# Block 0 by halves of the heads, and block 2's q and k transposes ahead of its V

## The chip, the cores and the metric

The kernel runs on one core of a Trainium2 chip. The core has a matrix engine (TensorE, PE in the profile, with its weight loads shown as PEld), a vector engine (VectorE, DVE), a scalar engine (ScalarE, ACT), GpSimd (POOL) and SyncE (SP), which here only issues transfers. Each engine works through its own list in order; semaphores order them against each other. Transfers run on 16 DMA engines that all issuing engines share. The metric is the device time of one execution in microseconds, and the median of the runs is compared.

## The reference

```python
# q, k, v: [8 batches, 8 heads, 576 tokens, 64], float32
q_c, k_c, v_c = (x.reshape(B, H, 9, 64, D) for x in (q, k, v))     # chunks of 64 tokens
scores = np.matmul(q_c, k_c.transpose(0, 1, 2, 4, 3)) / np.sqrt(D)
attn = np.exp(scores - np.max(scores, axis=-1, keepdims=True))
attn = attn / (np.sum(attn, axis=-1, keepdims=True) + 1e-09)
x = np.matmul(attn, v_c)                 # -> [4608 tokens, 512], heads side by side
h = np.maximum(x @ w_in, 0.0)            # w_in: [512, 2048]
out = h * h @ w_out                      # w_out: [2048, 512]
```

Attention runs only inside chunks of 64 tokens; then every token passes through two large products with a squared ReLU between them.

## The kernel before

**Tiling.** The 4608 tokens are cut into 18 groups of 256 (four chunks of one batch; the left-over chunks form two groups of their own), and two groups make a block of 512 tokens. The attention of a block must be done before its input projection, which goes over 16 d_ff tiles of 128 (each with four matmuls over d_model, `dt` 0 to 3); the output projection follows. The attention of later blocks is woven into the projections of earlier ones by hand: a loop hands out *slots*, one for each d_ff tile or output step, and a table `plan` says which attention steps, loads and sums come behind which slot. Blocks 0 to 3 use plain input projections; from block 4 on, and for most output projections, sums of operands replace one product in eight.

**One group's attention.** q and k arrive as float32, and TensorE reads the upper halves of the words as bf16. Groups 0 to 3 have q and k transposed on TensorE (`transpose_paired`, L400) and copied out of PSUM (L409); later groups have them cast on POOL (`cast_q`, `cast_k`, L449 and L454) and transposed by a DMA (`transpose_qk_dma`, L460). `scores` (L483) multiplies keys by queries and ACT takes the exponential (L494). `values` (L510) multiplies by V, which has a column of ones for the sums; DVE takes reciprocals (L442) and scales (L443). `transpose_x` (L540) or `transpose_x_early` (L521) brings x into the layout `xT` of the projection.

**PSUM.** Banks come round robin from two pools: `ps_ffn` with four, and the attention's two double banks (`att_bank`), which alternate.

**Block 0** has nothing to hide behind, and is written out before the slot loop. SP's list begins with q and k of groups 0 and 1, each 512 KB in runs of two rows of 64 (512 B), then V in 9 pieces, then w_in in eight loads of 256 columns (L329), each cast to bf16 on POOL (L334; the second half of the first on ACT, L333), then w_out (L339). PE goes through the two groups one behind the other, with `keep_busy` matmuls (L433, their result unused) in the gaps, and starts the input projection (`ffn_in`, L579) with d_ff tiles 0 and 1 on the first 256 tokens, then on the others, then goes on with 512 tokens at a time. ACT applies the ReLU (L590), and DVE or ACT squares (L598, L596).

**The slots of blocks 0 and 1.** In block 0's loop the q, k and V of block 2 (groups 4 and 5) are issued in the first 17 slots. In block 1's loop group 4 is cast at slot 16 and group 5 at slot 20 (`C`), their transposing DMAs come at 21 and 25 (`TD`), scores at 36 and 37, values at 38 and 40. As SP's list runs in order, the order of these lines is the order of the transfers.

## Time and profile before

| | |
|---|---|
| median of 3 runs | 277.18 us (277.12 to 279.81) |
| the profiled execution | 276.91 us, its span 275.1 us |
| busy over the span | PE 264.9 us (96%), DVE 199.2, ACT 168.3, POOL 89.6 |
| moved by DMA | 55.60 MB, mean 202 GB/s |
| chain that ended last | PE 87%, DMA 4%, SP's list 3%, DVE 3%, ACT 1% |

The span runs from the first to the last instruction of one execution. A profile row gives start and length in us, the engine, the line of the kernel, the operation, what it writes and reads with the shape, and in brackets how long the engine had been idle and what ended that. "PE busy" counts pipelined matmuls whose ends are modelled, so it is read together with the time per matmul.

### The profile page before, as it was taken

To read this page: it belongs to the slowest core of one execution; us is meant where nothing else is said; L and a number is where in the kernel's file an instruction comes from. 1 tells how busy PE (TensorE), PEld (TensorE's weight loads), DVE (VectorE), ACT (ScalarE), POOL (GpSimd) and SP (SyncE) were. 2 spreads that over 40 slices of the span, in tenths; PEclk is the share of its full clock that TensorE was granted. 3 is DMA by queue.
4 is the path that set the end of the run, shared out by engine and by line. 5 is a ranking of instruction groups with operands and counts; after the bars stand their busy time and mean duration, and the time that the engine had idled before them with its cause. 6 is when DMAs were issued, how large, how long until landed. Compare 5 with 4: busy or idle time off the path is not lost.

```text
span 275.1 us, 7923 instructions
## 1 busy us (share of the span) xinstructions
PE 264.9 (96%) x3261; PEld 203.4 (74%) x3261; DVE 199.2 (72%) x365; ACT 168.3 (61%) x300; POOL 89.6 (33%) x122
## 2 busy tenths in 40 slices
PE   2999999999999999999999999999999999999995
PEld 2764445888774588447878888888888888888884
DVE  1457514999538592499989998799779877994752
ACT  1657614894458883877678765565746665756430
POOL 2048834240360012040245224551643212331600
PEclk9999999999999999999999999999999999999999
DMA  7999999999999999999999999697999530220223
GB/s 216 262 352 389 361 332 270 339 213 172 262 210 218 238 234 218 275 223 178 228 236 197 218 238 194 103 220 196 244 187 224 123 76 2 99 55 7 71 83 114
DMA packets 136056, 55.60 MB, mean 202 GB/s; under 512 B 104273, under 2 KB 131921, under 8 KB 136017
## 3 DMA queue, kind: packets, MB, share of 16 engines
q1 hardware_dynamic: 133248, 46.54, 74.0%
q0 software_dynamic: 2624, 8.39, 9.6%
q8 instruction: 26, 0.43, 0.6%
q10 hardware_dynamic: 144, 0.13, 0.1%
q14 instruction: 14, 0.11, 0.1%
HBM read 36.70 MB, written 9.44 MB: 168 GB/s over the span
## 4 chain that ended last, share of the span: by engine, by line
PE 87%; DMA 4%; SPq 3%; DVE 3%; ACT 1%; issue 1%; ACTq 0%; DVEq 0%
PE ps_ffn L657 22%; PE ps_out L780 22%; PE ps_ffn L579 17%; PE ps_ffn L780 14%; PE ps_ffn L901 5%; PE ps_att L510 3%; PE ps_att L540 2%; DMA vo_sb<-in_v_dram 2%; PE ps_att L483 2%; DMA xT<-x 2%; DVE gT L598 2%; SPq L266 1%; SPq L308 1%; SPq L312 1%; DVE x L443 1%; ACT e L494 1%
## 5 line engine op out<-in xcount | busy, mean ns | idle before, releaser
L579 PE MATMUL ps_ffn<-xT,w_in_bf 128*128 128x512 bf16 (+1 forms) x328 | 57.8, 333 | 0.0
L780 PEld LDWEIGHTS <-w_st 128*128 128x128 bf16 x512 | 48.9, 98 | 6.6 <-DVE w_st L614 0.5
L665 DVE CUSTOM_DVE_ANT_0 relu<-ps_ffn,w_st 128x512 f32<-128x512 f32 x60 | 39.3, 684 | 13.0 <-PE ps_ffn L657 11.6
L579 PEld LDWEIGHTS <-w_in_bf 128*128 128x128 bf16 x328 | 31.2, 98 | 21.6 <-POOL w_in_bf L334 0.2
L598 DVE TENSOR_TENSOR gT<-relu 128x256 bf16<-128x256 bf16 (+2 forms) x68 | 34.1, 537 | 17.8 <-ACT relu L590 17.3
L590 ACT ACTIVATE relu<-ps_ffn 128x256 bf16<-128x256 f32 (+2 forms) x82 | 39.4, 501 | 9.4 <-PE ps_ffn L579 8.6
L657 PE MATMUL ps_ffn<-qk_st,w_in_bf 128*128 128x256 bf16 x240 | 35.3, 273 | 0.1
L657 PEld LDWEIGHTS <-w_in_bf 128*128 128x128 bf16 x320 | 30.7, 98 | 4.1 <-issue 0.3
L809 POOL DMA_DIRECT2D out_dram<-o_sb x24 | 17.6, 733 | 43.6 <-DVE o_sb L614 23.3
L780 PEld LDWEIGHTS <-gT 128*128 128x128 bf16 x296 | 28.6, 98 | 3.3
L780 PE MATMUL ps_out<-w_out_bf,w_st 128*128 128x256 bf16 x240 | 30.8, 273 | 0.0
L699 ACT ACTIVATE w_st<-ps_ffn 128x512 f32<-128x512 f32 x20 | 11.9, 597 | 29.6 <-PE ps_ffn L657 29.6
L443 DVE TENSOR_TENSOR x<-ps_att,recs 128x512 bf16<-128x512 f32 x36 | 24.9, 692 | 1.2
L657 PEld LDWEIGHTS <-qk_st 128*128 128x128 bf16 x240 | 22.6, 98 | 3.2 <-DVE qk_st L614 0.3
L657 PE MATMUL ps_ffn<-xT,qk_st 128*128 128x256 bf16 x160 | 23.9, 273 | 0.0
L676 POOL TENSOR_TENSOR qk_st<-relu 128x512 bf16<-128x512 f32 x10 | 10.3, 1034 | 41.6 <-DVE relu L665 38.1
L494 ACT ACTIVATE e<-ps_att 128x1024 bf16<-128x1024 f32 x18 | 18.3, 1025 | 8.5 <-PE ps_att L483 8.5
L676 POOL TENSOR_TENSOR gT<-relu 128x512 bf16<-128x512 f32 x10 | 10.3, 1033 | 35.4 <-DVE relu L665 30.5
L449 POOL CAST qkb<-qk_st 128x1024 bf16<-128x1024 f32 x12 | 13.0, 1082 | 14.9 <-DMA qk_st<-in_q_dram 14.9
L674 ACT ACTIVATE gT<-relu 128x512 bf16<-128x512 f32 x28 | 17.7, 631 | 0.0
L780 PE MATMUL ps_ffn<-w_out_bf,w_st 128*128 128x256 bf16 x144 | 17.7, 273 | 0.0
L614 DVE TENSOR_TENSOR w_st<-gT,w_st 128x1024 bf16<-128x1024 bf16 x26 | 16.8, 682 | 0.0
(92 smaller groups left out, 428.7 us busy)
## 6 DMA issues: line engine op xcount, KB each, us to landing
qk_st<-in_q_dram SPq DMA_DIRECT2D x16, 512.0 KB, 5.6
out_dram<-o_sb POOLq DMA_DIRECT2D x28, 256.0 KB, 3.9
qk_st<-in_k_dram SPq DMA_DIRECT2D x24, 256.0 KB, 5.6
ve_sb<-in_v_dram SPq DMA_DIRECT2D x32, 128.0 KB, 3.9
w_st<-in_moe_w_in_dram SPq DMA_DIRECT2D x8, 512.0 KB, 5.9
w_st<-in_moe_w_out_dram SPq DMA_DIRECT2D x8, 512.0 KB, 5.5
vo_sb<-in_v_dram SPq DMA_DIRECT2D x24, 128.0 KB, 3.6
qk_st<-in_k_dram SPq DMA_DIRECT2D x4, 512.0 KB, 5.8
```

What stands on the lines that cost most here:

```text
L443: nc.vector.tensor_tensor(out=x, in0=o[:, :, :, 0:D], in1=rec.to_broadcast([128, 2, n, D]), op=ALU.mult)
L494: nc.scalar.activation(out=e_out, in_=s_in, func=AF.Exp, scale=scale)
L579: nc.tensor.matmul(out=h[:, 0:n], lhsT=w_in_bf[:, dt, ft * 128:(ft + 1) * 128], rhs=xT[:, c // 128:(c + n) // 128, dt, :], start=(dt == 0) ...
L590: nc.scalar.activation(out=rl[:, 0:n], in_=h[:, 0:n], func=AF.Relu)
L598: nc.vector.tensor_tensor(out=dst, in0=src, in1=src, op=ALU.mult)
L614: nc.vector.tensor_tensor(out=out, in0=in0, in1=in1, op=op)
L657: nc.tensor.matmul(out=bank[:, f * GT:(f + 1) * GT], lhsT=a[:, dt, ft * 128:(ft + 1) * 128], rhs=b[:, :, dt, :], start=(first and f == 0 a ...
L665: nc.vector._custom_dve(TENSOR_ADD_SAT, out=out, in0=in0, in1=in1, s0=BIG, s1=0.0)
L674: engine.activation(out=dst, in_=r, func=AF.Square)
L676: engine.tensor_tensor(out=dst, in0=r, in1=r, op=ALU.mult)
L780: nc.tensor.matmul(out=out_ps, lhsT=lhsT, rhs=b[:, i, :], start=(first and i == 0 and (last or t == 0)), stop=(i == HF - 1), skip_group_ch ...
L809: dma.dma_start(out=out[t0:t0 + GT, col:col + HD].rearrange("(t p) d -> p t d", p=128), in_=o_sb.rearrange("p (t d) -> p t d", d=HD))
```

## The change

Block 0 is no longer done by its two groups of 256 tokens with all 8 heads, but by two halves of the heads (4 each) with all 512 tokens. For each half, q and k are loaded with four rows of 64 in a run (1 KB), V in 9 pieces of four heads, and w_in's first 512 columns in two halves of 256 rows, one behind each half's V. x of the first half of the heads is rows 0 to 255 of the projection's contraction (`dt` 0 and 1), so the first four d_ff tiles have these two matmuls done (`first_tile`) between the steps of the second half; `dt` 2 and 3 and the ReLU and square follow in `first_in` when the second half is done. Tile 3 of block 0 is squared on DVE in place of ACT. PE's fillers in the second half write into free columns of the attention's banks (`fill`).

In block 1's slots, the transposing DMAs of block 2 move from 21 and 25 to 16 and 20, directly behind their casts, and V of each of the two groups, until now issued in block 0's slots, comes behind its group's transpose, at 18 and 22.

```diff
@@ -312,10 +312,7 @@
             odd.append(lambda n=n, p=p, m=m, b=b, s=s: nc.sync.dma_start(
                 out=v_odd[n % NO][p:p + m, :, 0:D],
                 in_=v[b, 1::2, s:s + m, :].rearrange("h s d -> s h d")))
-        if g < 2:
-            yield from [even[0], *odd[:-1], even[1], odd[-1]]
-        else:
-            yield from even + odd
+        yield from even + odd
 
     def go(pieces):
         for f in pieces:
@@ -329,8 +326,6 @@
         nc.sync.dma_start(out=st, in_=moe_w_in[:, cols].rearrange("(a p) f -> p a f", p=128))
         n = 256 // n_cast
         for c in range(0, 256, n):
-            if i == 0 and c:
-                return lambda: nc.scalar.copy(out=w_in_bf[:, :, c:c + n], in_=st[:, :, c:c + n])
             nc.gpsimd.tensor_copy(
                 out=w_in_bf[:, :, i * 256 + c:i * 256 + c + n], in_=st[:, :, c:c + n])
 
@@ -514,18 +509,119 @@
                             start=True, stop=True)
             out_of_x(x[:, t].rearrange("p h a d -> p a h d"), ps, n_hp)
 
-    def transpose_x_early(g, t):
...
+    NH, HH = 2, H // 2
+
+    def half_loads(half):
+
+        b, s0 = chunks[0][0]
+        hs = slice(HH * half, HH * half + HH)
+
+        def rows(which, src):
+            return lambda: nc.sync.dma_start(
+                out=loaded(half, which).rearrange("p (h e) -> p h e", h=HH),
+                in_=src[b, hs, s0:s0 + BT, :].rearrange("h (s i) d -> s h (i d)", i=4))
+
+        def even(t):
+            s = s0 + 128 * t
+            return lambda: nc.sync.dma_start(
+                out=v_even[t // 2][:, t % 2, NH * half:NH * half + NH, 0:D],
+                in_=v[b, HH * half:HH * half + HH:2, s:s + 128, :].rearrange("h s d -> s h d"))
+
+        def odd(n):
+            p0, p1 = (CH if n == 0 else 0), (CH if n == 4 else 2 * CH)
+            s = s0 + 128 * n - CH + p0
+            return lambda: nc.sync.dma_start(
+                out=v_odd[n][p0:p1, NH * half:NH * half + NH, 0:D],
+                in_=v[b, HH * half + 1:HH * half + HH:2, s:s + p1 - p0, :].rearrange(
+                    "h s d -> s h d"))
+
+        return [rows(0, q), rows(1, k), even(0), even(1), odd(0), odd(1), odd(2), even(2), even(3),
+                odd(3), odd(4)]
+
+    def load_w_in_half(r):
+        st = w_st[next(n_staged) % 5].rearrange("p (a f) -> p a f", a=2)
+        nc.sync.dma_start(
+            out=st, in_=moe_w_in[256 * r:256 * r + 256, 0:512].rearrange("(a p) f -> p a f", p=128))
+        for c in (0, 256):
+            nc.gpsimd.tensor_copy(
+                out=w_in_bf[:, 2 * r:2 * r + 2, c:c + 256], in_=st[:, :, c:c + 256])
+
+    def transpose_half(half, which, bank):
...
+        qkT = state["half", half]
+        psb = bank.bitcast(BF16)[:, 0:1024].rearrange("c (h i q) -> c h i q", h=NH, i=4)
+        src = loaded(half, which).bitcast(BF16).rearrange("p (h i d) -> p h i d", h=HH, i=4)
+        for hp in range(NH):
+            for i in range(4):
+                for a in range(2):
+                    nc.tensor.transpose(
+                        out=psb[64 * a:64 * a + 64, hp, i, :],
+                        in_=src[:, 2 * hp + a, i, 1::2],
+                        identity=ident)
+        for hp in range(NH):
+            copy = nc.vector.tensor_copy if hp or not which else nc.scalar.copy
+            copy(out=qkT[:, which, hp].rearrange("c (p i) -> c p i", i=4),
+                 in_=psb[:, hp].rearrange("c i p -> c p i"))
+
+    def scores_half(half):
+        qkT = state["half", half]
+        ps = att_bank()
+        for hp in range(NH):
+            for t in range(4):
+                for a in range(2):
+                    for p in range(2):
+                        c = p ^ a
+                        o0 = a * 512 + hp * 256 + t * 64
+                        cols = slice((2 * t + p) * CH, (2 * t + p + 1) * CH)
+                        nc.tensor.matmul(
+                            out=ps[64 * c:64 * c + 64, o0:o0 + 64],
+                            lhsT=qkT[64 * a:64 * a + 64, 1, hp, cols],
+                            rhs=qkT[64 * a:64 * a + 64, 0, hp, cols],
+                            start=True, stop=True)
+        e = e_tile()
+        state["e half", half] = e.rearrange("p (a h t q) -> p a h t q", a=2, h=NH, t=4)
+        nc.scalar.activation(out=e, in_=ps, func=AF.Exp, scale=scale)
+
+    def values_half(half, u, n_fill=0):
+        e = state["e half", half]
...
+        x = state["x half", half]
+        ps = att_bank().rearrange("p (a f) -> p a f", a=2)
+        fill(n_fill, ps[:, 0, 384:512])
+        for tt in range(2):
+            t = 2 * u + tt
+            for hp in range(NH):
+                for a in range(2):
+                    for p in range(2):
+                        c = p ^ a
+                        vb = (v_odd[t + p] if a else v_even[t // 2][:, t % 2]).bitcast(BF16)
+                        o0 = (tt * NH + hp) * (D + 1)
+                        nc.tensor.matmul(
+                            out=ps[64 * p:64 * p + 64, a, o0:o0 + D + 1],
+                            lhsT=e[64 * c:64 * c + 64, a, hp, t, :],
+                            rhs=vb[64 * c:64 * c + 64, NH * half + hp, 1::2],
+                            start=True, stop=True)
+        out_of_x(x[:, 2 * u:2 * u + 2].rearrange("p t h a d -> p a (t h) d"), ps, 2 * NH)
+
+    def transpose_x_half(half, u, bank, copy):
+        psb = bank.bitcast(BF16)[:, 0:512]
+        x = state["x half", half]
+        for n in range(2 * NH):
             nc.tensor.transpose(
+                out=psb[:, n * 128:n * 128 + 128],
+                in_=x[:, 2 * u + n // NH, n % NH].rearrange("p a d -> p (a d)"),
                 identity=ident)
+        copy(out=x_tile(0)[:, 2 * u:2 * u + 2, NH * half:NH * half + NH, :],
+             in_=psb.rearrange("p (t h q) -> p t h q", t=2, h=NH))
+
+    def fill(n, out):
+        for _ in range(n):
+            nc.tensor.matmul(out=out, lhsT=ident, rhs=ident, start=True, stop=True)
 
     def transpose_x(g):
@@ -570,8 +666,26 @@
 
     FT_ORDER = [*range(n_ft // 2, n_ft), *range(n_ft // 2)]
 
+    def squared(j, u, h, c, n, ft):
+        gT = gT_main.rearrange("p (u h) (f t) -> p u h f t", u=2, f=4)
...
+        nc.scalar.activation(out=rl[:, 0:n], in_=h[:, 0:n], func=AF.Relu)
+        u0, u1 = c // GT, (c + n) // GT
+        dst = gT[:, u0:u1, ft // 4, ft % 4, :]
+        src = rl[:, 0:n].rearrange("p (u t) -> p u t", t=GT)
+        if (n == 512 and ft in SQUARES_ON_ACT and (j or ft > 3)) or (n < 512 and ft in (12, 3)):
+            nc.scalar.activation(out=dst, in_=src, func=AF.Square)
+        else:
+            nc.vector.tensor_tensor(out=dst, in0=src, in1=src, op=ALU.mult)
+
     def ffn_in(j, parts):
-        gT = gT_main.rearrange("p (u h) (f t) -> p u h f t", u=2, f=4)
         xT = xTs[j]
         for u, (c, n, ft) in enumerate((c, n, ft) for c, n, fts in parts for ft in fts):
             h = ps_ffn.tile([128, 512], FP32, name="ps_ffn")
@@ -581,23 +695,27 @@
                     lhsT=w_in_bf[:, dt, ft * 128:(ft + 1) * 128],
                     rhs=xT[:, c // 128:(c + n) // 128, dt, :],
                     start=(dt == 0), stop=(dt == n_dt - 1))
...
-            if (n == 512 and ft in SQUARES_ON_ACT) or (
-                    n < 512 and ft in (12, 3)) or (j == 0 and u == 0):
-                nc.scalar.activation(out=dst, in_=src, func=AF.Square)
-            else:
-                nc.vector.tensor_tensor(out=dst, in0=src, in1=src, op=ALU.mult)
+            squared(j, u, h, c, n, ft)
             yield
 
+    first_h = []
+
+    def first_tile(ft, dts):
+        if dts[0] == 0:
+            first_h.append(ps_ffn.tile([128, 512], FP32, name="ps_ffn"))
+        for dt in dts:
+            nc.tensor.matmul(
+                out=first_h[ft],
+                lhsT=w_in_bf[:, dt, ft * 128:(ft + 1) * 128],
+                rhs=xTs[0][:, :, dt, :],
+                start=(dt == 0), stop=(dt == n_dt - 1), skip_group_check=True)
+
+    def first_in():
+        for ft in range(4):
+            first_tile(ft, (2, 3))
+            squared(0, ft, first_h[ft], 0, BT, ft)
+            yield
+        yield from ffn_in(0, [(0, BT, range(4, n_ft))])
 
 
     a11, a12 = w_in_bf[:, 0:2, 0:d_ff // 2], w_in_bf[:, 2:4, 0:d_ff // 2]
@@ -964,33 +1082,40 @@
     def AV1(g):
         values(g, [1])
 
-    HT = BT // 2
-    go(pieces([0, 1]))
-    cast_first = load_w_in(0, n_cast=2)
-    TE(0)
-    transpose_qk(1, ps_ffn, None)
-    SC(0)
-    transpose_qk(1, None, ps_ffn)
+    def ffn_bank():
+        return ps_ffn.tile([128, 512], FP32, name="ps_ffn")
+
+    act = nc.scalar.copy
+    go(half_loads(0))
+    load_w_in_half(0)
+    go(half_loads(1))
+    load_w_in_half(1)
+    transpose_half(0, 0, ffn_bank())
+    transpose_half(0, 1, ffn_bank())
     keep_busy(8)
-    AV(0, [0])
-    SC(1)
-    keep_busy(6)
-    AV(0, [1])
-    transpose_x_early(0, 0)
-    keep_busy(10)
-    transpose_x_early(0, 1)
-    AV(1, [0])
-    AV(1, [1])
+    scores_half(0)
+    keep_busy(8)
+    values_half(0, 0)
+    values_half(0, 1)
     keep_busy(4)
-    transpose_x_early(1, 0)
-    cast_first()
-    keep_busy(8)
-    transpose_x_early(1, 1)
-    first_ffn_in = ffn_in(0, [(0, HT, (0, 1)), (HT, HT, (0, 1)), (0, BT, range(2, n_ft))])
-    next(first_ffn_in)
-    next(first_ffn_in)
-
-    for i in range(1, 8):
+    transpose_x_half(0, 0, ffn_bank(), act)
+    transpose_half(1, 0, ffn_bank())
+    transpose_x_half(0, 1, ffn_bank(), act)
+    first_tile(0, (0, 1))
+    transpose_half(1, 1, att_bank())
+    for ft in range(1, 4):
+        first_tile(ft, (0, 1))
+    scores_half(1)
+    values_half(1, 0, 8)
+    values_half(1, 1, 4)
+    both = att_bank()
+    fill(8, both[:, 256:384])
+    transpose_x_half(1, 0, both[:, 0:256], act)
+    fill(6, both[:, 256:384])
+    transpose_x_half(1, 1, both[:, 512:768], nc.vector.tensor_copy)
+    first_ffn_in = first_in()
+
+    for i in range(2, 8):
         load_w_in(i, n_cast=2 if i < 5 else 1)
     for i in range(5):
         load_w_out(i)
@@ -1009,7 +1134,7 @@
             plan.setdefault(slot, []).append((f, x))
 
         if j == 0:
-            loads, go_slots = pieces(far), range(17)
+            loads, go_slots = itertools.chain(*map(qk_pieces, far)), range(17)
             at(28, summed(b11_p_b21, b11, b21))
             for slot, f in ((24, TA), (27, SC), (29, AV), (31, XT)):
                 at(slot, f, nxt[0])
@@ -1022,9 +1147,10 @@
             for slot, f in ((3, SC), (6, AV), (12, XT)):
                 at(slot, f, grps[1])
             for i, g in enumerate(nxt):
-                for slot, f in ((16 + 4 * i, C), (21 + 4 * i, TD), (36 + i, SC), (38 + 2 * i, AV),
+                for slot, f in ((16 + 4 * i, C), (16 + 4 * i, TD), (36 + i, SC), (38 + 2 * i, AV),
                                 (41 + 2 * i, XT)):
                     at(slot, f, g)
+                at(18 + 4 * i, lambda g=g: go(v_pieces(g)))
             for i, g in enumerate(far):
                 at(36 + 4 * i, C, g)
                 at(42 + 3 * i, TD, g)
```

34 lines of the change are left out of this document (15 added, 19 removed).

## The prediction

> **What bounds the kernel now.** I read the page first: its span, and the rows of its 40 slices for TensorE (PE) and for the DMA engines.
>
> ```profile
> span 275.1 us, 7923 instructions
> ...
> PE   2999999999999999999999999999999999999995
> ...
> DMA  7999999999999999999999999697999530220223
> ```
>
> PE and the DMA engines both look full over most of the span, so the digits don't say which one sets the end. The busy times by stretch do, cut where block 0's first projection starts (17.46) and ends (31.47), and before the last stores.
>
> ```profile
> 17.46:31.47 14.01, 14.01 (x73) 7.17 (x74) 10.04 (x14) 10.84 (x22) 11.88 (x14) 1.00 1.06 379
> 31.47:260.00 228.53, 228.16 (x2841) 177.54 (x2840) 176.18 (x327) 146.84 (x262) 74.12 (x83) 1.00 0.85 193
> 260.00:275.10 15.10, 11.72 (x107) 10.05 (x104) 6.86 (x14) 3.14 (x9) 1.45 (x3) 1.00 0.36 110
> ```
>
> The columns are the length, then the busy time of PE, its weight loads, DVE (VectorE), ACT (ScalarE) and POOL (GpSimd). Of 228.53 us behind 31.47, PE is busy 228.16. A busy PE need not run at its peak, so I take the third view, the chain that ended last.
>
> ```profile
> 17.46 14.01 PE ps_ffn L579 x72
> 31.47 7.77 PE ps_ffn L901 x36
> ```
>
> 36 matmuls of 512 columns in 7.77 us are 0.216 us each. At that pace 64 such matmuls take 13.8 us, and the 64 tiles' worth of block 0's input projection took 14.01: PE runs without a gap from 17.46 on. So what a change of the opening is worth is how far it moves the moment at which this unbroken run of PE work reaches its 31.47, and a change behind that is worth something only where PE would wait.
>
> **The opening now.** I follow it in order of time.
>
> ```profile
> 4.77 1.06 PE L400 MATMUL ps_ffn<-ident,qk_st 128*64 128x128 bf16 x16 [4.77 <-DMA qk_st<-in_q_dram]
> 5.88 1.29 DVE L409 COPY qkT<-ps_ffn 128x512 bf16<-128x512 bf16 x2 [5.88 <-PE ps_ffn L400]
> 6.26 1.06 PE L400 MATMUL ps_ffn<-ident,qk_st 128*64 128x128 bf16 x16 [0.42 <-DMA qk_st<-in_k_dram]
> ...
> 8.74 0.64 PE L483 MATMUL ps_att<-qkT 64*64 64x64 bf16 x32
> 9.44 1.02 ACT L494 ACTIVATE e<-ps_att 128x1024 bf16<-128x1024 f32 x1 [1.00 <-PE ps_att L483]
> 10.36 1.03 PE L433 MATMUL ps_ffn<-ident 128*128 128x128 bf16 x8
> 11.32 0.30 PEld L510 LDWEIGHTS <-e 64*64 64x64 bf16 x16 [0.20 <-issue]
> 11.84 0.21 DVE L442 RECIPROCAL recs<-ps_att 128x8 f32<-128x8 f32 x1 [1.70 <-PE ps_att L510]
> 12.08 0.69 DVE L443 TENSOR_TENSOR x<-ps_att,recs 128x512 bf16<-128x512 f32 x1
> ...
> 16.30 0.69 DVE L443 TENSOR_TENSOR x<-ps_att,recs 128x512 bf16<-128x512 f32 x1
> 16.63 0.58 ACT L526 COPY xT<-ps_ffn 128x512 bf16<-128x512 bf16 x1 [1.38 <-PE ps_ffn L521]
> 17.05 0.40 PE L521 MATMUL ps_ffn<-ident,x 128*128 128x128 bf16 x4
> 17.48 0.42 DVE L526 COPY xT<-ps_ffn 128x512 bf16<-128x512 bf16 x1 [0.49 <-PE ps_ffn L521]
> ```
>
> The projection starts at 17.46 on the first 256 tokens, while the last copy of x for the others is still to come (17.48 to 17.90). The steps behind each arrival are thus partly covered now; in the new order the last group's steps are not.
>
> **When the data arrive.** The loads run in the order of SyncE's (SP's) list; the weight casts on POOL show their landings.
>
> ```profile
> 16.79 0.61 POOL L334 CAST w_in_bf<-w_st 128x512 bf16<-128x512 f32 x1 [14.59 <-DMA w_st<-in_moe_w_in_dram]
> 18.11 1.17 POOL L334 CAST w_in_bf<-w_st 128x512 bf16<-128x512 f32 x2 [0.70 <-DMA w_st<-in_moe_w_in_dram]
> 19.46 2.67 POOL L334 CAST w_in_bf<-w_st 128x512 bf16<-128x512 f32 x4 [0.18 <-DMA w_st<-in_moe_w_in_dram]
> ...
> 6.00:8.00 2.00, 1.31 (x22) 1.07 (x24) 1.17 (x2) 0.63 (x2) 0.00 (x0) 1.00 1.15 348
> 10.00:12.00 2.00, 2.00 (x65) 1.63 (x60) 0.30 (x2) 1.54 (x3) 0.00 (x0) 1.00 1.43 224
> ```
>
> 512 KB of q or k in runs of 512 B take 1.49 us (q at 4.77, k at 6.26). 512 KB of w_in in runs of 1 KB take 1.33 (16.79, 18.11, 19.46). V in runs of 256 B is slower: the last rows have 348 GB/s with q and k and 224 with V. From k of group 1 (6.26 and two more steps, 9.24) to the first w_in less its own 1.33 (15.46), 1 MB of V took 6.2 us. The change reads q and k by four heads in runs of 1 KB, so I price them at w_in's 1.33; V keeps its 256 B, 3.1 per half. Starting from 4.77 - 1.49 = 3.28, the new order lands q 4.61, k 5.94, V 9.04, w_in rows 0 to 255 10.37, then for half 1 q 11.70, k 13.03, V 16.13, and w_in rows 256 to 511 17.46. That is 0.65 ahead of the 18.11 of now for the same bytes. The Trainium skill (DMA: Bandwidth & Descriptors, Specifications) puts line rate at runs of 512 B and up; by that the longer runs of q and k gain nothing, and the start of the projection worked out below would be some 0.5 us later. The two rows, 1.49 against 1.33, speak for a small gain, and I keep it.
>
> SP must issue twice as many V pieces, 18 for 9, each of half the size.
>
> ```profile
> 0.75 0.45 SPq L266 DMA_DIRECT2D qk_st<-in_q_dram  x1
> ...
> 10.73 0.60 SPq L312 DMA_DIRECT2D vo_sb<-in_v_dram  x1
> ...
> 60.47 0.37 SPq L312 DMA_DIRECT2D vo_sb<-in_v_dram  x1
> ```
>
> An issue takes from 0.37 to 0.60 with 0.06 behind it. At 0.52 in all, SP is through V of half 0 at 6.6, through k of half 1 at 8.1 and V of half 1 at 12.8, and issues the second w_in half by 13.3: always ahead of the stream above. I take that, and keep 0.66 for a rival.
>
> **Block 0, step by step.** Half 0: k 5.94, 16 transposes 1.06, to 7.00; the two copies (0.65 each, now one on ACT and one on DVE) lie beside the 8 filling matmuls (1.03, to 8.03); scores start, exp 0.70 later (8.74 to 9.44), 1.02 long, to 9.75; the values then, reciprocal 0.52 behind their start (11.32 to 11.84), product 0.24 behind that, 0.69 long: 11.20; the second values' reciprocal and product follow on DVE, 0.03 + 0.24 + 0.69: 12.16. From here the machine is at its faster pace: the trace shows 128-column matmuls at 0.129 us at 10.36 and 0.072 at 13.32, and the same work later at
>
> ```profile
> 13.32 0.72 PE L433 MATMUL ps_ffn<-ident 128*128 128x128 bf16 x10
> ...
> 16.43 0.61 PE L433 MATMUL ps_ffn<-ident 128*128 128x128 bf16 x8
> ...
> 42.88 0.45 PE L483 MATMUL ps_att<-qkT 64*64 64x64 bf16 x32
> 43.38 1.02 ACT L494 ACTIVATE e<-ps_att 128x1024 bf16<-128x1024 f32 x1 [2.02 <-PE ps_att L483]
> ...
> 48.23 0.61 PE L400 MATMUL ps_ffn<-ident,qk_st 128*64 128x128 bf16 x16
> ```
>
> PE's list goes on with q of half 1: 11.70 + 0.61 = 12.31, just past the product; x of half 0's second part transposed, ACT's copy 0.44 behind its start and 0.58 long: 13.33. Only now can the first d_ff tile's two matmuls run (13.35 to 13.78), and behind them k of half 1, there since 13.03: to 14.39. Then the other three tiles' six matmuls, 1.30, to 15.69, which cover the copies of k (15.05). Scores 15.69; exp 0.50 later (42.88 to 43.38), to 17.21; values 17.25; reciprocal 17.77; products to 18.70 and 19.66; transposes 19.71; copy 0.43 behind their start, 0.42 long: **the projection proper starts at 20.6**, with w_in's casts long done (17.46 + two of 0.61). V of half 1 (16.13) is not what it waits for.
>
> Eight of its 64 matmuls are done by then. The remaining 56 at 0.216 take 12.1 and end at 32.7, against 31.47: **1.2 us later**. Break-even is a start at 19.4. What is gained (1.7 us of PE work laid into waiting time) is less than what is exposed: half 1's chain from scores to copy, 4.9 us in which PE has only filling matmuls. Nothing behind is late for it: w_in's third load lands near 18.8 and is needed at 22.3. The square of tile 3 moves from ACT to DVE and tile 0's comes to DVE whole, beside 12 us of PE work; DVE is busy 10.04 of 14.01 us in this stage, so I count nothing. Without that room it would be one pass over 128x512, near the copy's 0.42.
>
> **Block 2's transposes ahead of V.** SP's list now has V of groups 4 and 5 (to 61.6) ahead of the two transposing DMAs.
>
> ```profile
> 54.67 1.04 POOL L454 CAST qkb<-qk_st 128x1024 bf16<-128x1024 f32 x1 [2.69 <-DMA qk_st<-in_k_dram]
> 58.86 1.17 POOL L454 CAST qkb<-qk_st 128x1024 bf16<-128x1024 f32 x1 [1.61 <-DMA qk_st<-in_k_dram]
> ...
> 61.66 6.17 SPq L460 DMA_TRANSPOSE qkT<-qkb  x2
> ...
> 70.15 0.44 PE L483 MATMUL ps_att<-qkT 64*64 64x64 bf16 x32
> ...
> 73.93 0.22 PE L510 MATMUL ps_att<-ve_sb,e 64*64 64x65 bf16 x2
> ...
> DMA to landing us min/median/max: 2.4/3.9/7.2
> ```
>
> New: the first transpose waits for its cast (55.7) and issues to 58.8 (half of 6.17); behind it on SP wait five V pieces (near 0.55 each, 61.6), the second transpose (its cast ends 60.0, so no wait; 64.7) and four V pieces (66.9), then block 3's q and k, which before start at 67.9. No queue but SP's is passed, and nothing ends later on it. The last V piece lands at the median 3.9 behind its issue (66.4 + 3.9 = 70.3), at the longest 7.2 (73.6), and is used at 73.93 + 1.2. PE doesn't wait here before (scores at 70.15 directly behind the matmuls), so nothing is to gain: 0, from 0 to 0.8 lost with both the longest issue and landing. A gain needs a PE wait that isn't there.
>
> Sum: +1.2 us on the profiled execution's 276.91 (275.1 of span, 1.8 around it). It lies 0.27 under the median of the runs, 277.18; on that the forecast is **278.4**.
>
> **Rivals.**
> (a) Not slower: the DMA stream, not PE, sets what follows. Place: the loads from 17 to 200 us; price: they come 0.65 earlier, so 277.18 - 0.65 = **276.5**; it decides if PE's idle time behind 31.47 is over 1.2 us, so that the later start vanishes in waits. For it: the DMA row is at 9. Against: only 0.37 us of idle there. 0.07.
> (b) SP's issues bind. At 0.66 each, V of half 1 is issued to 15.5 and the second w_in half at 16.1; with q's 4.0 from issue to landing (0.75 to 4.77) that lands at 20.1, and the last V at up to 19.4 (3.9), 1.7 us late for the second values: **280.1**. For it: 0.60 at 10.73; against: 0.37 and 0.45 where fewer are outstanding. 0.13.
> (c) The half chain meets the slower pace: PE has more pauses between 10.5 and 13.5, and the first tiles are matmuls on the path. With 0.129 / 0.072 = 1.8 times on 8 of 0.216 (1.4 more), two sets of transposes (0.45 each) and the scores (0.64 for 0.45): 2.5 more, **280.9**. Against: the pauses in which PE waits for x and V now, from 13.3 to 16.4, left its pace as it was (0.072 at 13.32, 0.076 at 16.43). 0.10. The Trainium skill (TensorE: Matmul & The Clock Gate, Part 1) has a gate that opens after some 3.4 us of sustained work and shuts after an idle window as long; the trace agrees with the opening (slow at 10.36, fast at 13.32), and no run here shows a shutting.
> (d) The reordering doesn't do what it says: transposes come no earlier and V late, a wait of 0.8 at the values: **279.2**. 0.05.
>
> **How the numbers follow.** Forecast 0.62 (starts from 19.9 to 21.3 by 0.7 us of landings and gaps, 277.7 to 279.1), (a) 0.07, (b) 0.13, (c) 0.10, (d) 0.05, the rest 0.03 on either side. The range 276.5 to 280.8 takes in all but most of (c), half of (a) and the rest. About 1%, 2.8 us, is what a measurement here tells from no change: slower than 279.95 is half of (b), nearly all of (c) and little else, 0.17; faster than 274.4 has no case of its own, 0.02; within 1% 0.81.
>
> **What would show it.** Block 0's projection starting its second halves near 20.6, PE idle or filling from 16.2 to 20.1; first d_ff tile near 13.4; output projection from 32.7; the first block-2 transpose issued near 56; PE without gaps behind. The forecast is wrong if the second halves start before 19.4, if k of half 1 lands past 14, or if PE waits between 60 and 80.

## The result and the profile after

The changed kernel takes 284.75 us (median of 6 runs, 283.71 to 286.13) where the kernel before, on the same chip, takes 277.35 (6 runs, 276.47 to 279.81): 1.0257 times as long, 95% interval 1.0208 to 1.0307. The forecast was 278.4 with a range to 280.8. The profiled execution after took 283.71 us, 6.8 more than the one before (276.91). Here and below, medians and ranges are of all runs of a kernel, while ratios leave out the runs that fell into a slower state.

The chain that ended last and the stretches cut at the same events as in the prediction (start of the second halves of block 0's projection, start of the output projection, last stores) put all of the loss ahead of 25.86. The chain leads back to the load of q of half 1, issued at 7.64 and landed at 13.66:

```profile
7.64 6.02 DMA qk_st<-in_q_dram
...
25.86 1.89 PE ps_ffn L707 x8
```

The last three columns of a stretch are TensorE's granted clock (1.00 is full), the DMA share and GB/s.

```profile
25.86:37.95 12.09, 12.09 (x57) 5.48 (x57) 10.77 (x13) 9.14 (x16) 9.32 (x9) 1.00 0.98 339
37.95:260.00 222.05, 221.08 (x2776) 171.36 (x2778) 171.26 (x320) 143.47 (x255) 69.86 (x77) 1.00 0.87 196
```

The 56 matmuls of 512 columns take 12.09 us without a gap, and the output projection starts at 37.95, where the trace before has 31.30 for the same matmuls in the same view: 6.65 us later. Behind that point PE is idle 0.97 us in 222.05 (0.37 in 228.53 before). PE's last instruction ends 6.87 us later than before (278.59 against 271.72), so the remaining 0.2 us is all that the rest of the program adds. What has to be explained is why the second halves started at 25.86 and not at 20.6.

PE's timeline of the opening (start, length, engine, line, and in brackets the idle time before with what ended it):

```profile
13.71 1.06 PE L559 MATMUL ps_ffn<-ident,qk_st 128*64 128x128 bf16 x16 [1.62 <-DMA qk_st<-in_q_dram]
14.70 0.61 PE L615 MATMUL ps_ffn<-ident,x 128*128 128x128 bf16 x4
15.98 1.01 PE L707 MATMUL ps_ffn<-xT,w_in_bf 128*128 128x512 bf16 x2 [0.67 <-ACT xT L619]
16.93 1.06 PE L559 MATMUL ps_att<-ident,qk_st 128*64 128x128 bf16 x16
17.92 2.18 PE L707 MATMUL ps_ffn<-xT,w_in_bf 128*128 128x512 bf16 x6
20.04 0.45 PE L578 MATMUL ps_att<-qkT 64*64 64x64 bf16 x32
...
23.50 0.39 PE L615 MATMUL ps_att<-ident,x 128*128 128x128 bf16 x4
24.55 0.49 PE L624 MATMUL ps_att<-ident 128*128 128x128 bf16 x6 [0.67 <-ACT xT L619]
24.89 0.39 PE L615 MATMUL ps_att<-ident,x 128*128 128x128 bf16 x4
25.86 1.89 PE L707 MATMUL ps_ffn<-xT,w_in_bf 128*128 128x512 bf16 x8 [0.59 <-DVE xT L619]
```

Set against the prediction's steps:

| step | forecast | measured | later by |
|---|---|---|---|
| q of half 1 there | 11.70 | 13.7 | 2.0 |
| its transposes over | 12.31 | 14.70 | 2.4 |
| first d_ff tile | 13.35 | 15.98 | 2.6 |
| k of half 1 transposed | 14.39 | 17.92 | 3.5 |
| scores of half 1 | 15.69 | 20.04 | 4.35 |
| last transposes of x | 19.71 | 24.89 | 5.2 |
| second halves start | 20.6 | 25.86 | 5.26 |

Three losses stand in it. **Data**: 2.0 us, PE waits 1.62 us for q. **PE's pace**: 2.35 more up to the scores; 16 transposes take 1.06, not 0.61, two tile matmuls 1.01 (0.5 each, 0.216 later), and six 2.18, not 1.30. **A wait inside the chain**: from the first transposes of x (23.50) to the last (24.89) lie 1.4 us, because six filling matmuls first wait 0.67 us for ACT's copy and then run for 0.34; without them the last ones would follow at once, as soon as DVE's product is there (23.82 in DVE's timeline). That is 1.0 us, and the steps between give 0.1 back.

For the data, SP's timeline, SP's waits, the stretches, POOL's casts and two rows of the DMA view (the last figure is the time from issue to landing) belong together:

```profile
1.80 1.01 SPq L526 DMA_DIRECT2D ve_sb<-in_v_dram  x2
...
5.95 1.02 SPq L533 DMA_DIRECT2D vo_sb<-in_v_dram  x2
...
13.68 0.37 SPq L526 DMA_DIRECT2D ve_sb<-in_v_dram  x1
15.04 1.04 SPq L533 DMA_DIRECT2D vo_sb<-in_v_dram  x2
16.76 0.37 SPq L543 DMA_DIRECT2D w_st<-in_moe_w_in_dram  x1
```

```profile
SPq L533 <- DMA qk_st<-in_k_dram: 1.2, 2, 1.0
SPq L543 <- DMA ve_sb<-in_v_dram: 0.7, 1, 0.7
SPq L526 <- DMA qk_st<-in_q_dram: 0.6, 1, 0.6
```

```profile
6.00:8.00 2.00, 2.00 (x28) 1.63 (x32) 1.28 (x3) 0.59 (x1) 0.00 (x0) 1.00 0.69 145
8.00:10.00 2.00, 1.76 (x41) 1.29 (x40) 0.39 (x1) 1.02 (x1) 0.00 (x0) 1.00 0.76 169
...
9.00:11.50 2.50, 2.05 (x45) 1.46 (x44) 0.97 (x3) 0.95 (x1) 0.00 (x0) 1.00 0.96 228
...
16.00:18.00 2.00, 2.00 (x19) 0.99 (x19) 0.10 (x1) 0.00 (x0) 0.00 (x0) 1.00 0.38 72
```

```profile
11.91 1.17 POOL L546 CAST w_in_bf<-w_st 128x512 bf16<-128x512 f32 x2 [9.70 <-DMA w_st<-in_moe_w_in_dram]
21.43 1.17 POOL L546 CAST w_in_bf<-w_st 128x512 bf16<-128x512 f32 x2 [8.35 <-DMA w_st<-in_moe_w_in_dram]
```

```profile
w_st<-in_moe_w_in_dram SPq DMA_DIRECT2D x1, 512.0 KB, 4.9
vo_sb<-in_v_dram SPq DMA_DIRECT2D x1, 32.0 KB, 2.2
```

Nine V pieces of 64 KB (the half pieces 32) take SP from 1.80 to 6.97, 0.57 each, and the DMA share falls to 0.69 at 6 to 8 us, where before it was 1.15 (a share over 1 means packets overlapping). V of half 0 is not late by that: its last piece, issued at 6.36, landed 2.2 later, at 8.5, where the forecast had 9.04. Late is what stands behind it: the first half of w_in, issued at 7.00, landed 4.9 later, at 11.9 (forecast 10.37). From 9.0 to 11.5 the DMA engines were busy with it (a share of 0.96), but moved 228 GB/s; q behind it was to be there at 11.70 and came at 13.7.

Then SP itself waits for landings of transfers to which the waiting one has no relation in the program: the 21st transfer of the list (a V piece, 13.68) is released when the 13th (q of half 1) lands, the 22nd (15.04) by the 14th (k of half 1), the 24th (w_in's second half, 16.76) by the 16th. Each is eight places further back. So eight transfers of this list are under way at most, and small ones fill the places as well as large ones: at 16 to 18 us the DMA share is 0.38. The second half of w_in, issued at 16.76, was cast from 21.43, where the forecast had it issued by 13.3 and landing at 17.46.

### The profile page after: what moved, and what is told of

Read it like the earlier page. It is cut to its first block, busy times and chain, and to the rows that moved or that the text cites. A ratio compares the mean times of both kernels' runs of the same rounds, so it can differ in the third digit from the quotient of the medians.

```text
span 281.9 us, 7931 instructions
## 1 busy us (share of the span) xinstructions
PE 267.5 (95%) x3260; PEld 203.6 (72%) x3263; DVE 201.2 (71%) x367; ACT 165.7 (59%) x293; POOL 90.0 (32%) x123
## 4 chain that ended last, share of the span: by engine, by line
PE 88%; DMA 4%; DVE 4%; ACT 2%; SPq 1%; issue 1%; DVEq 0%; ACTq 0%
PE ps_ffn L775 22%; PE ps_out L898 22%; PE ps_ffn L693 15%; PE ps_ffn L898 13%; PE ps_ffn L1019 5%; PE ps_att L505 2%; DMA qk_st<-in_q_dram 2%; PE ps_ffn L707 2%; DVE gT L686 2%; PE ps_att L478 2%; PE ps_att L636 2%; DMA qk_st<-in_k_dram 2%; DVE x L438 1%; ACT e L489 1%; ACT relu L679 1%
## 5 line engine op out<-in xcount | busy, mean ns | idle before, releaser
L693 PE MATMUL ps_ffn<-xT,w_in_bf 128*128 128x512 bf16 (+1 forms) x304 | 54.4, 334 | 0.0
L783 DVE CUSTOM_DVE_ANT_0 relu<-ps_ffn,w_st 128x512 f32<-128x512 f32 x60 | 39.2, 684 | 13.4 <-PE ps_ffn L775 11.9
L686 DVE TENSOR_TENSOR gT<-relu 128x512 bf16<-128x512 bf16 (+2 forms) x68 | 35.5, 561 | 15.4 <-ACT relu L679 15.1
L679 ACT ACTIVATE relu<-ps_ffn 128x512 bf16<-128x512 f32 (+2 forms) x80 | 39.1, 511 | 10.5 <-PE ps_ffn L693 7.7
L693 PEld LDWEIGHTS <-w_in_bf 128*128 128x128 bf16 x304 | 28.9, 98 | 20.6
L775 PEld LDWEIGHTS <-w_in_bf 128*128 128x128 bf16 x320 | 30.6, 98 | 4.1 <-issue 0.3
L817 ACT ACTIVATE w_st<-ps_ffn 128x512 f32<-128x512 f32 x20 | 11.9, 597 | 29.6 <-PE ps_ffn L775 29.6
L489 ACT ACTIVATE e<-ps_att 128x1024 bf16<-128x1024 f32 x16 | 16.3, 1025 | 6.8 <-PE ps_att L478 6.8
L444 POOL CAST qkb<-qk_st 128x1024 bf16<-128x1024 f32 x12 | 12.9, 1078 | 11.4 <-DMA qk_st<-in_q_dram 11.4
```

The lines of the kernel that those rows point to most:

```text
L489: nc.scalar.activation(out=e_out, in_=s_in, func=AF.Exp, scale=scale)
L679: nc.scalar.activation(out=rl[:, 0:n], in_=h[:, 0:n], func=AF.Relu)
L686: nc.vector.tensor_tensor(out=dst, in0=src, in1=src, op=ALU.mult)
L693: nc.tensor.matmul(out=h[:, 0:n], lhsT=w_in_bf[:, dt, ft * 128:(ft + 1) * 128], rhs=xT[:, c // 128:(c + n) // 128, dt, :], start=(dt == 0) ...
L775: nc.tensor.matmul(out=bank[:, f * GT:(f + 1) * GT], lhsT=a[:, dt, ft * 128:(ft + 1) * 128], rhs=b[:, :, dt, :], start=(first and f == 0 a ...
L783: nc.vector._custom_dve(TENSOR_ADD_SAT, out=out, in0=in0, in1=in1, s0=BIG, s1=0.0)
```

## The experiments

"Start" below is the start of the second halves in the run's profile (25.86 after), "out0" that of block 0's output projection (37.95 after, 31.30 before); each ratio is to the kernel before on the same chip.

**Which part loses.** `part1_only` is the changed kernel with block 2's order put back; `part2_only` is the kernel before with block 2's order alone.

```diff
# part1_only, against after; part2_only makes the reverse edit on before
-            loads, go_slots = itertools.chain(*map(qk_pieces, far)), range(17)
+            loads, go_slots = pieces(far), range(17)
-                for slot, f in ((16 + 4 * i, C), (16 + 4 * i, TD), (36 + i, SC), (38 + 2 * i, AV),
+                for slot, f in ((16 + 4 * i, C), (21 + 4 * i, TD), (36 + i, SC), (38 + 2 * i, AV),
-                at(18 + 4 * i, lambda g=g: go(v_pieces(g)))
```

> The changed kernel with block 2's transposes and V put back as they were before; block 0 by halves is kept. Theory (the whole loss is in block 0's opening): within 0.5 us of the changed kernel's 284.75. Rival (the new order of block 2 in SyncE's list costs part of it): under 283, down to 278.4 if it costs all that the forecast left out.

> The kernel before with only block 2's transposes put ahead of V. Theory (PE has no wait there that a transpose could end): 277.3 within 0.5 us. Rival (V or the transposes now land late): over 279.

`part1_only`: 285.48 (284.31 to 287.32), 1.0278 [1.0222, 1.0334], start 25.98, out0 38.06. `part2_only`: 0.9994 [0.995, 1.0039]. The loss is block 0's alone, and the reordering is worth nothing that can be measured.

**The filling matmuls behind ACT's copy.** First they were sent to the other bank of the same two-bank tile, then the last two sets of transposes got a tile each, and the six fillers were left out.

```diff
# fills_apart
-    fill(6, both[:, 256:384])
+    fill(6, both[:, 896:1024])
# apart_tile
-    both = att_bank()
-    fill(8, both[:, 256:384])
-    transpose_x_half(1, 0, both[:, 0:256], act)
-    fill(6, both[:, 256:384])
-    transpose_x_half(1, 1, both[:, 512:768], nc.vector.tensor_copy)
+    one = att_bank()
+    fill(8, one[:, 256:384])
+    transpose_x_half(1, 0, one[:, 0:256], act)
+    transpose_x_half(1, 1, att_bank()[:, 0:256], nc.vector.tensor_copy)
```

> The changed kernel with the six filling matmuls between the last two x transposes written to the other PSUM bank of the same tile, so that they share none with the copy on ACT. Theory (PE's list is held 1.0 us by those fillers, which wait for ACT's copy): the last transposes start near 23.9 in place of 24.89, the projection's second halves 1.0 us earlier than 25.86, time 283.7. Rival (the product on DVE is what the last transposes wait for, or the fillers wait for the copy wherever they write): no change, 284.7.

> The changed kernel with the last two x transposes in two PSUM tiles in place of two parts of one, and without the six filling matmuls between them. Theory (what PE writes to a tile waits for ACT's copy out of it, whichever bank; in the fillers' new bank nothing had moved): the last transposes start right behind the product on DVE, 1.0 us earlier than 24.9 to 25.0; the second halves start near 24.9 in place of 25.9. If PE alone sets the rest: 283.7. If later loads set it: no gain, or less than 0.5. Rival (the transposes wait for something else): start near 25.9 as now.

`fills_apart` took 287.25 (284.13 to 288.35), 1.0333 [1.0273, 1.0392]; its PE timeline has the same wait:

```profile
24.67 0.49 PE L624 MATMUL ps_att<-ident 128*128 128x128 bf16 x6 [0.67 <-ACT xT L619]
```

The wait goes with the tile, not with the bank: the forecast of this experiment failed. `apart_tile` took 285.32 (284.61 to 286.05), 1.0237 [1.0179, 1.0294]. Its timeline of PE:

```profile
23.95 0.78 PE L615 MATMUL ps_att<-ident,x 128*128 128x128 bf16 x8
25.33 1.46 PE L707 MATMUL ps_ffn<-xT,w_in_bf 128*128 128x512 bf16 x6 [0.61 <-DVE xT L619]
...
134.10 1.91 PE L898 MATMUL ps_out<-w_out_sum,gT 128*128 128x256 bf16 x16 [1.49 <-ACT xT L641]
```

From the first transposes of x to the start it is 1.38 us, 2.36 after: the 1.0 us is the fillers with their wait, as held. The start came only 0.53 earlier, since PE's slow pace lasted longer in this run (the six tile matmuls took 2.74). And the time did not follow, because a new wait of 1.49 us stands at 134.10. The edit draws one attention bank more; banks alternate, so from then on every step has the other one, and the sums' tile, which takes one of the two over, waits for a copy out of it. `busy_apart2`, below, tests this.

**PE's pace.** Filling matmuls were put where PE waits for q of half 1 and for the copy of x.

```diff
# pe_busy
     transpose_x_half(0, 0, ffn_bank(), act)
+    keep_busy(16)
     transpose_half(1, 0, ffn_bank())
     transpose_x_half(0, 1, ffn_bank(), act)
+    keep_busy(8)
     first_tile(0, (0, 1))
```

> The changed kernel with 16 more filling matmuls ahead of q of half 1 and 8 more ahead of the first d_ff tile, where PE stood still. Theory (PE falls back to its slow pace while it waits for q): the first tiles' matmuls take 0.216 in place of some 0.43, k's transposes 0.61 in place of 1.06, the second halves start 1.2 to 1.7 us earlier, time 283.0 to 283.6. Rival (the landings of q and k alone set the time): no change, or 0.3 later for the added matmuls.

Its timeline, opening and block 3's attention:

```profile
10.28 0.40 PE L428 MATMUL ps_ffn<-ident 128*128 128x128 bf16 x4
...
11.54 1.91 PE L428 MATMUL ps_ffn<-ident 128*128 128x128 bf16 x16
13.52 1.06 PE L559 MATMUL ps_ffn<-ident,qk_st 128*64 128x128 bf16 x16
...
14.87 0.61 PE L428 MATMUL ps_ffn<-ident 128*128 128x128 bf16 x8
15.71 0.59 PE L707 MATMUL ps_ffn<-xT,w_in_bf 128*128 128x512 bf16 x2 [0.23 <-ACT xT L619]
16.23 0.64 PE L559 MATMUL ps_att<-ident,qk_st 128*64 128x128 bf16 x16
16.80 1.47 PE L707 MATMUL ps_ffn<-xT,w_in_bf 128*128 128x512 bf16 x6
...
24.03 1.89 PE L707 MATMUL ps_ffn<-xT,w_in_bf 128*128 128x512 bf16 x8 [0.59 <-DVE xT L619]
...
100.28 0.19 PE L505 MATMUL ps_att<-vo_sb,e 64*64 64x65 bf16 x1 [1.26 <-DMA vo_sb<-in_v_dram]
```

```profile
11.50:14.50 3.00, 2.94 (x35) 2.52 (x32) 0.54 (x1) 0.58 (x1) 1.17 (x2) 0.50 1.12 352
```

The granted clock is 0.50 from 11.5 to 14.5, and from 15 on it is full. Behind that the opening behaves as held: two tile matmuls 0.59 (1.01 after), 16 transposes 0.64 (1.06), six matmuls 1.47 (2.18), start 24.03, 1.83 us earlier. The time is not: 288.35 (285.5 to 291.8), 1.04 [1.0322, 1.0478]. In the profiled run (285.5) start to out0 takes 12.61 where the same matmuls took 12.09, and in the stretch behind, to 260 us, PE waits 1.5 us for V and 0.8 for transposes of block 3, which it doesn't do after. An opening that runs faster on loads that don't meets those loads further on. The other runs, some 3 us longer, have no trace, and what they add is open.

**The number of pieces.** V of block 0 in the 9 transfers of all eight heads, of twice the size, behind q and k of half 0. This changes the order too: all of V now stands ahead of w_in and of half 1's q and k.

```diff
# whole_v
-    go(half_loads(0))
+    go(half_loads(0)[:2])
+    go(v_pieces(0))
+    go(v_pieces(1))
     load_w_in_half(0)
-    go(half_loads(1))
+    go(half_loads(1)[:2])
     load_w_in_half(1)
```

> The changed kernel with V of block 0 in 9 transfers of 128 KB (two of 64 KB) with all heads, behind q and k of half 0, in place of 18 of half the size; the rest of the order stays (w_in rows 0 to 255, then q and k of half 1, then w_in rows 256 to 511). Theory (at most 8 transfers of SyncE's list are under way, and 8 small ones starve the DMA engines): the second w_in half lands near 17.5 to 18.5 in place of 21.4; q of half 1 lands near 14.8, k 16.1; from 6 to 18 us the DMA share is at 1.0 and over. The projection's second halves start some 1 us later (26 to 27), PE's end follows, near 285.5. Rival (the longer runs of q and k, or the half w_in loads, are what is slow): the second w_in half still lands at 20 or later.

Stretches and the casts of the two halves of w_in on POOL:

```profile
6.00:12.00 6.00, 5.01 (x99) 3.83 (x100) 2.68 (x6) 1.61 (x2) 0.00 (x0) 1.00 1.20 212
12.00:18.00 6.00, 2.59 (x29) 1.93 (x28) 2.08 (x4) 1.17 (x2) 1.17 (x2) 1.00 1.05 362
...
14.24 1.17 POOL L546 CAST w_in_bf<-w_st 128x512 bf16<-128x512 f32 x2 [12.04 <-DMA w_st<-in_moe_w_in_dram]
18.56 1.17 POOL L546 CAST w_in_bf<-w_st 128x512 bf16<-128x512 f32 x2 [3.16 <-DMA w_st<-in_moe_w_in_dram]
```

In the same stretches the changed kernel has shares of 0.80 and 0.78 with 198 and 208 GB/s. The same bytes in half as many V pieces bring the second half of w_in 2.9 us earlier: its lateness goes with the number of pieces. That of the first half does so only in part. SP issued it at 8.11, while V's packets still filled the engines; V's last piece landed at 11.5 (issued at 7.42, 4.1 to landing), and the first half of w_in 2.7 later, at 14.2, where the forecast has 1.33 for it. The second half followed k of half 1 (17.3) in 1.2. The kernel as a whole loses, 289.9 (287.53 to 292.01), 1.0426 [1.0347, 1.0504], since q of half 1 now stands behind all of V and comes at 15.56 (start 27.56).

**The two together, and with V whole.** `busy_apart` has the edits of `pe_busy` and `apart_tile`; `busy_apart_v` has `whole_v`'s too; `busy_apart2` is `busy_apart` with one more bank drawn, so that the alternation is the old one.

```diff
# busy_apart_v, against busy_apart (with whole_v's edit)
-    keep_busy(16)
+    keep_busy(28)
# busy_apart2, against busy_apart
     transpose_x_half(1, 1, att_bank()[:, 0:256], nc.vector.tensor_copy)
+    att_bank()
```

> The fillers that keep PE's pace (as in pe_busy) and the last transposes in two tiles (as in apart_tile), V still in 18 pieces. Both theories have the second halves start near 23.0. If PE alone sets the rest: 281.8. If loads that come late set it: PE waits in block 0's projection for w_in and between 90 and 105 us for transposes or V of block 3, and the time is 284 or more.

> As busy_apart, with V of block 0 in 9 transfers as in whole_v, and 28 fillers for 16 since q of half 1 comes later. Second halves start near 24. If the loads' lateness is what holds busy_apart, it is gone here: no wait for w_in in block 0's projection, none between 90 and 105, time 282.5 to 283.5, below busy_apart in spite of the later start. If PE alone sets the rest: 1 us above busy_apart.

> busy_apart with one more PSUM bank drawn (and left unused), so that the attention's two banks alternate in later blocks as in the changed kernel. Theory (the 1.5 us wait of the output projection for ACT's copy near 132 came from the odd number of banks drawn): that wait is gone, time 1.5 us under busy_apart's 284.5 of the profiled execution, near 283.0. Rival (that wait is of the earlier start): it stays.

| | time (runs) | ratio [95%] | start | start to out0 |
|---|---|---|---|---|
| busy_apart | 287.41 (284.5 to 289.92) | 1.0341 [1.0265, 1.0417] | 23.03 | 13.08 |
| busy_apart_v | 285.58 (283.63 to 287.9) | 1.0224 [1.0135, 1.0312] | 24.68 | 12.09 |
| busy_apart2 | 284.36 (282.75 to 287.66) | 1.0278 [1.0191, 1.0365] | 23.09 | 13.56 |

PE's timeline of `busy_apart`, then of `busy_apart2`:

```profile
23.03 1.90 PE L707 MATMUL ps_ffn<-xT,w_in_bf 128*128 128x512 bf16 x8 [1.04 <-POOL w_in_bf L546]
25.74 10.53 PE L693 MATMUL ps_ffn<-xT,w_in_bf 128*128 128x512 bf16 x48 [0.81 <-ACT relu L679]
```

```profile
26.28 10.53 PE L693 MATMUL ps_ffn<-xT,w_in_bf 128*128 128x512 bf16 x48 [1.31 <-POOL w_in_bf L329]
...
131.26 1.91 PE L898 MATMUL ps_out<-w_out_sum,gT 128*128 128x256 bf16 x16
```

With PE's two losses mended the weights are the next bound: in `busy_apart` the second halves start only when w_in's second half is being cast (from 22.36), and in both kernels PE waits again in front of the later tiles, by the rows for the ReLU in `busy_apart` and for the weights in `busy_apart2`. With V whole these waits are gone (12.09), and the program is no slower although it starts 1.65 us later. The 1.49 us wait, which `busy_apart` has again (at 132.43), is gone in `busy_apart2`: it came from the alternation of the banks, not from the opening. `busy_apart2`'s profiled run took 282.75, 1.0 us less than after; over all its runs no gain can be told from the changed kernel's 284.75.

**Another list for half the pieces.** The ten odd V pieces of both halves were issued from ACT's list at the start; `mended` has this with `busy_apart2`'s edits, and `mended_order` also transposes k of half 1 ahead of the first tile and lays two tiles behind the scores.

```diff
# two_lists (odd V pieces)
-            return lambda: nc.sync.dma_start(
+            return lambda: nc.scalar.dma_start(
...
+    for half in range(2):
+        go([f for i, f in enumerate(half_loads(half)) if i in (4, 5, 6, 9, 10)])
...
# mended_order, against mended
-    first_tile(0, (0, 1))
     transpose_half(1, 1, att_bank())
-    for ft in range(1, 4):
+    for ft in range(2):
         first_tile(ft, (0, 1))
     scores_half(1)
-    values_half(1, 0, 8)
+    for ft in range(2, 4):
+        first_tile(ft, (0, 1))
+    values_half(1, 0, 2)
```

> The changed kernel with the ten odd-head V pieces of block 0 issued from ScalarE's list at the start in place of SyncE's; the same 18 pieces of the same sizes. Theory (SyncE's issue time and its limit of 8 transfers under way starve the DMA engines): the second w_in half is issued before 11 and lands by 18.5 in place of 21.4; q of half 1 lands near 13.2, k 14.5; the DMA share from 6 to 18 us is back at 1.0 and over. The second halves start 0.5 us earlier than 25.9, time 284 or a little less. Rival (pieces of 64 KB are slow in the DMA engines themselves): the second w_in half lands at 20 or later.

> All three together: fillers that keep PE's pace, last transposes in two tiles (with the bank count kept even), odd-head V pieces on ScalarE's list. By the terms of the forecast's own sum, with q of half 1 landing near 13.2 and not 11.7: second halves start near 22.2, no wait for w_in, time 277.4 + (22.2 - 19.4) = 280.2. If something else sets the end: 282 or more.

> As mended, with k of half 1 transposed ahead of the first d_ff tile, and two of the four tiles' first halves laid behind the scores, beside the exponential. The path then has neither the first tile ahead of k's transposes nor two tiles ahead of the scores: second halves start some 0.6 to 1.2 us earlier than in mended, near 21.3, time near 279.3. Slower than the kernel before's 277.4 by the chain from scores to copy, which no order hides.

`two_lists` took 290.02 (287.98 to 291.62), 1.0455 [1.0367, 1.0544], start 28.57. It is no clean test. ACT is busy issuing until 8.28 and copies k of half 0 late, so the scores of half 0 come at 10.24 (7.93 after); and SP's third transfer goes out only when q of half 0 has landed, with ACT's transfers under way beside it:

```profile
0.75 7.53 ACTq L533 DMA_DIRECT2D vo_sb<-in_v_dram  x10
...
4.77 3.45 SPq L526 DMA_DIRECT2D ve_sb<-in_v_dram  x4
```

The second half of w_in was cast from 19.83, between the bounds of the two theories. Up to 4.77 SP had two transfers of its own under way and ACT six, eight together: this speaks for places that both lists share. `mended` took 284.88 (283.87 to 287.02), 1.0278 [1.0205, 1.035]; ACT's issuing holds half 0 back by 2.2 us (scores at 10.12), so its start is 25.53 and not 22.2: a miss. But it has no wait for w_in: start to out0 12.09. `mended_order` took 283.78 (283.21 to 284.46), 1.0224 [1.0174, 1.0273], start 24.88. The order of the steps moves the start by 0.65 us, and its median is the shortest of the family, still 2% longer than before. No start in any run was earlier than 23.03, and the prediction's break-even is 19.4.

## Why the prediction was wrong

The sum 1.2 us was made of a start at 20.6 and 12.1 us behind it. The second was right (12.09). The start was wrong by 5.26, in three steps.

**"At 0.52 in all, SP ... always ahead of the stream above", and 1.33 for half of w_in.** This step failed first. In the stream one term was far off, both times that it stands there:

| | landing: forecast | measured | behind the one before: forecast | measured |
|---|---|---|---|---|
| V of half 0 | 9.04 | 8.5 | 3.1 | 2.6 |
| w_in rows 0 to 255 | 10.37 | 11.9 | 1.33 | 3.3 |
| q of half 1 | 11.70 | 13.7 | 1.33 | 1.8 |
| k of half 1 | 13.03 | 15.0 | 1.33 | 1.4 |
| V of half 1 | 16.13 | 18.1 | 3.1 | 3.1 |
| w_in rows 256 to 511 | 17.46 | 21.4 | 1.33 | 3.3 |

The 1.33 was read from loads of w_in that follow one another; here each half follows V in small pieces. SP has a part in this. It issued the first half at 7.00, while the engines were running dry, and q of half 0, with nothing ahead of it, took 3.8 us from its issue (0.75) to its landing: by that row the half could not be there before 10.8. The prediction compared SP's time with the stream without the time between issue and landing. It also read issues of 0.37 to 0.60 us, where the third to the fifth of the trace before took 1.39 to 1.45. But in `whole_v`, where SP was well ahead, this half still took 2.7 us behind V. The forecast's prices put q at 14.8 in that order, and it came at 15.56, 0.8 late; so some 1.2 of the 2.0 us go with the pieces or the order. Why half of w_in moves so slowly behind V is open: its other half, of the same size, took 1.2 behind k in `whole_v`.

Rival (b) named SP's issues, with the consequence in V of half 1 and w_in, and there it was near: V of half 1 was issued to 16.07 (it had 15.5), and the second half of w_in landed at 21.4 (20.1). But PE's loss was ahead of that, at q of half 1. What neither had is the limit of eight transfers under way, which the trace before could not show, since SP has no such wait in its first 16 us there. The size of the runs of q and k was priced rightly enough: k of half 0 follows q by 1.39 us (4.58 and 5.97 in PE's timeline), between the 1.33 taken and the 1.49 of before. The Trainium skill's rule for runs of 512 B (DMA: Bandwidth & Descriptors, Specifications) would have 1.49; the trace lies between the two, and the difference is 0.1 us.

**"From here the machine is at its faster pace."** This step failed too, and rival (c) came true beside (b), at nearly the size it gave (2.5; measured 2.35). The argument against it was the trace before, where pauses left the pace as it was. But there PE had worked more, 2.00 of 2.00 us from 8 to 10 and again from 10 to 12:

```profile
8.00:10.00 2.00, 2.00 (x60) 1.72 (x58) 1.15 (x2) 1.00 (x2) 0.00 (x0) 1.00 1.26 289
```

After, it was busy 1.76 of the 2.00 from 8 to 10, with a wait of 1.62 soon behind, and in the profiled execution the pace had not risen. In `part1_only`, whose opening is the same, it had risen, and it fell again:

```profile
10.35 0.40 PE L428 MATMUL ps_ffn<-ident 128*128 128x128 bf16 x4
...
13.45 1.07 PE L559 MATMUL ps_ffn<-ident,qk_st 128*64 128x128 bf16 x16 [1.73 <-DMA qk_st<-in_q_dram]
...
14.00:19.50 5.50, 4.83 (x37) 2.38 (x34) 1.98 (x3) 1.17 (x2) 0.00 (x0) 0.50 0.56 125
```

Four fillers in 0.40 are the fast pace, the transposes behind the wait for q are at the slow one, and the granted clock is 0.50 up to 19.5. Either way the steps of half 1 met the slow pace, and both kernels start near 25.9. The rows tell when it rises. After, PE works on from 15.98 without a gap, and the last two of the six tile matmuls, seen in a narrow stretch of its timeline, are the first at the fast pace:

```profile
19.51 0.59 PE L707 MATMUL ps_ffn<-xT,w_in_bf 128*128 128x512 bf16 x2
```

In `pe_busy` PE works on from 11.25; the 16 transposes at 13.52 still take 1.06, and the fillers at 14.87 have the fast 0.076 each. Both are some 3.5 us of unbroken work. The Trainium skill (TensorE: Matmul & The Clock Gate, Part 1) asks for some 3.4 us of sustained work before the gate opens; the trace agrees. It also has the gate shut after an idle window as long, and here the measurement decides otherwise: in `pe_busy` the four fillers at 10.28 took 0.40 and the clock was at 0.50 from 11.5, though PE had no wait over 0.6 us from 8 to 11.4. The prediction took the fast pace, once reached, as kept; short waits were enough to lose it.

**"Transposes 19.71; copy 0.43 behind."** The six fillers between the two sets of transposes write the tile that ACT is copying from, and wait for it: with their wait they cost 1.0 us that no rival had (`apart_tile`: 1.38 against 2.36). I read those fillers as cover, not as instructions with a wait of their own.

What held: that the second half's chain from scores to copy, and not V, is what the start waits for (scores to start 5.8 us, 4.9 forecast, the 1.0 of the fillers being the difference); the direction; and block 2's part at nothing, with PE's waits behind 37.95 at 0.5 and two of 0.2 us, and the first transposing DMA at 62.64, which is the forecast's 56 and the 6.65 us by which everything moved. Rival (a), a DMA stream that sets what follows, is not what happened, but it is the next bound: `pe_busy` and `busy_apart` run into it as soon as the opening is faster.

What stays open: why half of w_in takes 3.3 us behind V, what sets the eight places, and what the runs of `pe_busy` without a trace add.

## What to carry to other kernels

When a load is cut into more pieces, lay the issues beside the stream piece by piece, with the time from issue to landing: each small piece takes an issue and holds a place among those under way. A price read from loads that follow one another need not hold for the same bytes behind small pieces. Count PE's pace from its last long stretch of unbroken work, and take the granted clock from several runs; a new wait early in a program costs its length and the slow pace of what follows, and fillers there must write to a tile that nobody is reading. A faster opening is worth only what the loads behind it allow, so look for the next wait before pricing it.

## What the runs showed of the hardware

- At most eight transfers were under way: the 21st, 22nd and 24th of SP's list went out on the landing of the 13th, 14th and 16th, with the DMA engines at a share of 0.38 at the end. In `two_lists` SP waited with two of its own and six of ACT's under way. Whether the chip or the program's semaphores set it was not tried.
- The first half of w_in (512 KB in rows of 512 columns) landed 3.3 us behind V in 64 KB pieces (228 GB/s at a DMA share of 0.96), 2.7 behind V in 128 KB pieces, and its other half 1.2 behind k (both in `whole_v`).
- TensorE's clock fell after short waits: in `pe_busy` it was 0.50 from 11.5 to 14.5 us, though PE had no wait over 0.6 us from 8 to 11.4. 128-column matmuls took 0.119 us there (16 in 1.91) and 0.076 at full clock (8 in 0.61).
- A granted clock of 1.00 does not prove the fast pace: in the changed kernel's profile the column is at 1.00 throughout the opening, while 16 transposes take 1.06 us up to 18.0 and 0.61 to 0.64 at the fast pace (`pe_busy`, 16.23).
- A matmul into one bank of a two-bank tile waited 0.67 us for a copy out of the other bank (`fills_apart`). Transposes into a tile of their own ran on without a wait (`apart_tile`, where the fillers are left out). Whether the hardware or the program's semaphores ask for it was not tried.
